# A two-layer feed-forward kernel behind local attention: the second layer's operand tiles get gaps of 32 to 192 bytes between them

## The chip, the cores and the metric

The kernel runs on one core of a Trainium2 chip. The metric is the device time of one execution in microseconds (us); lower is better. Engines go by the short names of the profile: PE is TensorE's matmul, PEld its load of the stationary operand, DVE VectorE, ACT ScalarE, POOL GpSimd, SP SyncE (it issues the DMAs).

## The reference

Local attention with a few global keys (2 sequences of 768 positions, 8 heads of 64), then two feed-forward layers on 1536 tokens of 512 features. Cut to what matters here:

```
x   = attention(q, k, v)                    # 1536 x 512, causal, 96 local and 8 global keys
h   = x @ w_in                              # 512 -> 1024
s   = h * softmax(h)
x   = layernorm(s) * g_ln @ w_out           # 1024 -> 512, the first layer
xn  = x / rms(x) * rms_g
out = (silu(xn @ w_gate) * (xn @ w_val)) @ w2_out    # 512 -> 1536 -> 512, the second layer
```

All is float32. The weights arrive as 64-bit floats and are made into float32 on the core, by bit operations.

## The kernel before, in words

The tokens go through in 12 units of 128 rows. Attention and the first layer run unit by unit, software-pipelined: an order written out by hand in a long string starts it off, and `slot` goes on with it. From about 242 us the second layer alone is left, with tokens in three groups of four units (`GRP` = 4, `NG` = 3), so that a group is 512 tokens wide.

To keep float32 accuracy, each operand is split into a high part that TensorE's faster float32r form holds, and a low part that is the rest: three matmuls, high x high, high x low and low x high, stand in place of one. So each tile comes as a pair: `xgh`/`xgl` (normalized tokens of a group, transposed), `w2hi`/`w2lo` (a slice of second-layer weights: gate, value and output), `ahi`/`alo` (the activated product).

The second layer: `gate_val(f, g)` multiplies weight slice f (12 of them) with token group g: 2 x 4 x 3 = 24 matmuls of 512 columns at L628. There the `w2` block of 128 columns is the stationary operand and `xg` the moving one. ACT takes a tanh of the gate, DVE two products (`th`), ACT rounds `th` to `ahi`, and POOL subtracts to get `alo`. `out_mm(f, g)`, one step later, multiplies the result with the output weights: 4 x 3 = 12 matmuls of 512 columns at L652, here with blocks of `ahi`/`alo` stationary and `w2` moving. With 12 slices and 3 groups that is 36 x 36 = 1296 matmuls. Slices go in three sweeps of four; the weights of the next ones are loaded (`ws`), converted (`wc`) and split meanwhile.

The order on PE is the order of the code (`manual_schedule`). A matmul's stationary block is loaded while the matmul before it streams its moving operand.

Where tiles lie in a partition is set by pools, stacked from two sides: the left stack grows upward, the right one downward. Nearly every tile is a multiple of 512 bytes long, so tiles that follow each other start at the same remainder mod 512. Only constants and small statistics tiles (`p_st`) shift it, and three pads (`PAD_G`, `PAD_X`, `PAD_R`) shift it back. By the sizes in the code, in the kernel before every operand tile of both layers, left and right, starts at remainder 32 mod 512; `ident`, the moving operand of the transposes, starts at 128. A block within a tile starts a multiple of 512 bytes from the tile's start. The pool `p_xg` on the left holds groups 0 and 1, whose space serves earlier as staging of first-layer weights (`wsh`, `wsl`, `wch`, `wcl`); `p_xg2`, `p_ws`, `p_wc`, `p_a` and `p_w2a` (weight slices 0 and 1) lie on the right, where attention's tiles were; `p_w2b` (the other slices) lies on the left, where the first layer's weights were.

Of the kernel before, what the change touches and what calls it, by code (L numbers as in the profile page):

```python
# [12 lines left out]
F32 = mybir.dt.float32  # L13
F32R = mybir.dt.float32r
BF16 = mybir.dt.bfloat16
I32 = mybir.dt.int32
U32 = mybir.dt.uint32
# [5 lines left out]
P = 128  # L23
# [4 lines left out]
KD = DM // P  # L28
# [5 lines left out]
GRP = 4  # L34
NG = NU // GRP
# [1 line left out]
NLOC = 97  # L37
SWEEPS = [4, 4, 4]
MASK = 1.0e12
PAD_G, PAD_X, PAD_R = 128, 384, 448  # L40
LEAD = 1
LAG = 2
DLAG = 3
# [60 lines left out]
CW = 512  # L104
# [14 lines left out]
class Kernel:  # L119
# [485 lines left out]
        self.w2[f] = (hi, lo)  # L605

    def alloc_group(self, g, pool):
        self.xg[g] = [
            pool.tile([P, KD, GRP * P], F32R, tag=f"xg{t}{g}", name=f"xg{t}{g}") for t in ("h", "l")
        ]  # L610

    def silu_mul(self, a, g, v):
        nc = self.nc
# [4 lines left out]
    def gate_val(self, f, g, parts=(0, 1)):  # L618
        nc = self.nc
        xh, xl = self.xg[g]  # L620
        wh, wl = self.w2[f]
        for t in parts:
            pp = self.ps.tile([P, GRP * P], F32, tag=("h", "s")[t], name="gv")
            n = 0
            for k in range(KD):
                c = slice((t * KD + k) * P, (t * KD + k + 1) * P)
                for w, a in ((wh, xh), (wh, xl), (wl, xh)):
                    nc.tensor.matmul(pp, w[:, c], a[:, k, :], start=(n == 0), stop=(n == 3 * KD - 1))  # L628
                    n += 1
            self.gv[f, g, t] = pp  # L630
        if 1 not in parts:
            return
        th = self.p_a.tile([P, GRP * P], F32, tag="th", name="th")
        self.silu_mul(th, self.gv.pop((f, g, 0)), self.gv.pop((f, g, 1)))
        hi = self.p_a.tile([P, GRP * P], F32R, tag="ahi", name="ahi")
        lo = self.p_a.tile([P, GRP * P], F32R, tag="alo", name="alo")
        self.split(hi, lo, th, nc.gpsimd)
        self.act[f, g] = (hi, lo)
# [37 lines left out]
    def fast(self):  # L676
        tc, nc = self.tc, self.nc
        self.qk, self.v, self.p, self.xps, self.x = {}, {}, {}, {}, {}
        self.h, self.hst, self.ln, self.lT, self.xn = {}, {}, {}, {}, {}
        self.eps, self.gv = {}, {}  # L680
        self.sp, self.sst, self.w1, self.lps = {}, {}, {}, {}
        self.w2, self.act, self.acc, self.xg, self.pT = {}, {}, {}, {}, {}
        with ExitStack() as top:
            en = top.enter_context
            pools = {t: en(tc.tile_pool(name="ps_" + t, bufs=n, space=PSUM)) for t, n in BANKS.items()}
            self.ps = Banks(pools)
            self.pad(top, "left", PAD_G)
            self.p_xg = en(tc.tile_pool(name="p_xg", bufs=1, side="left"))
            self.early = (
                [self.p_xg.tile([P, 2, CW, 2], U32, tag=f"xg{t}0", name=f"ws{t}") for t in ("h", "l")],  # L690
                [self.p_xg.tile([P, 4, CW], U32, tag=f"xg{t}1", name=f"wc{t}") for t in ("h", "l")],
            )
            self.n_early = 0
            self.p_st = en(tc.tile_pool(name="p_st", bufs=DLAG + 1, side="left"))
            self.pad(top, "left", PAD_X)
            self.p_xn = en(tc.tile_pool(name="p_xn", bufs=2, side="left"))
            w1x = en(ExitStack())
            atx = en(ExitStack())
            we = w1x.enter_context
            ae = atx.enter_context  # L700
            self.p_w1 = we(tc.tile_pool(name="p_w1", bufs=1, side="left"))
            self.p_x = we(tc.tile_pool(name="p_x", bufs=LEAD + 1, side="left"))
            self.p_e = we(tc.tile_pool(name="p_e", bufs=LAG + 1, side="left"))
            self.p_sq = we(tc.tile_pool(name="p_sq", bufs=1, side="left"))
            self.p_l = we(tc.tile_pool(name="p_l", bufs=2, side="left"))
            self.pad(top, "right", PAD_R)
            self.p_bias = ae(tc.tile_pool(name="p_bias", bufs=1, side="right"))
            self.p_v = ae(tc.tile_pool(name="p_v", bufs=2, side="right"))
            self.p_qk = ae(tc.tile_pool(name="p_qk", bufs=4, side="right"))
            self.p_p = ae(tc.tile_pool(name="p_p", bufs=4, side="right"))  # L710
            self.p_pt = ae(tc.tile_pool(name="p_pt", bufs=4, side="right"))
            self.phase1()
            with tc.manual_schedule(engines={mybir.EngineType.PE}):
                atx.close()
                w2x = en(ExitStack())
                right = lambda n, b: w2x.enter_context(tc.tile_pool(name=n, bufs=b, side="right"))
                self.alloc_group(NG - 1, right("p_xg2", 1))
                self.p_ws = right("p_ws", 2)
                self.p_wc = right("p_wc", 2)
                self.p_a = right("p_a", 2)  # L720
                self.p_w2a = right("p_w2a", 2)
                self.phase2(w1x, w2x)
            w2x.close()
# [346 lines left out]
```

## Time and profile before

| | |
|---|---|
| median of 3 runs | 561.47 us (558.71 to 561.99) |
| profiled execution, its time | 558.16 us |
| its span, first to last instruction | 556.3 us |
| PE busy | 527.8 us, 95% of the span |
| granted TensorE clock, mean | 0.990 |
| matmuls of the second layer | 1296 of 512 columns |

The profile is that of one execution. The time is some 1.9 us longer than the span. A matmul's own duration (some 0.39 us for 512 columns) is a latency, of which the next matmul hides a part; the pace of PE is read from the starts of matmuls that follow each other.

### The profile page before, as it was taken

The numbers are of one execution on the slowest core, as the hardware profiler recorded it, in microseconds if no ns is written. First come the engines' busy times: TensorE is split into PE (matmuls) and PEld (weight loads), VectorE is DVE, ScalarE is ACT, GpSimd is POOL, SyncE is SP. The second block draws the span as 40 slices with busy tenths as digits, with TensorE's granted clock in tenths as the row PEclk, the third lists the DMA queues.
The fourth block names the chain that finished last, engine by engine and source line by source line (L and its number), as shares of the span: only waits on it lengthen the run. The fifth ranks groups of instructions, "written<-read, shape, count | busy, mean of one in ns | idle before, by whom it ended". The sixth has DMA issues, their size and how long they took to land.

```text
span 556.3 us, 7639 instructions
## 1 busy us (share of the span) xinstructions
PE 527.8 (95%) x2736; PEld 424.1 (76%) x2736; DVE 333.4 (60%) x797; ACT 236.6 (43%) x557; POOL 179.0 (32%) x207
## 2 busy tenths in 40 slices
PE   4788989999999999999998999999999999999994
PEld 3466767777877878888886888888888887888883
DVE  6989999776577558975787121673213788231312
ACT  5678767664466456643434121431112434111110
POOL 4874243311331232313544110541111545211010
PEclk9979999999999999999999999999999999999998
DMA  8864712231131022330444000240000242020202
GB/s 290 254 240 142 247 31 67 95 95 47 51 94 39 1 76 77 115 113 16 140 148 151 1 0 1 75 151 1 1 0 1 75 151 77 0 77 0 77 0 82
DMA packets 16670, 45.93 MB, mean 83 GB/s; under 512 B 1904, under 2 KB 2928, under 8 KB 16624
## 3 DMA queue, kind: packets, MB, share of 16 engines
q1 hardware_dynamic: 16624, 45.36, 24.3%
q8 instruction: 23, 0.38, 0.3%
q14 instruction: 23, 0.19, 0.1%
HBM read 42.21 MB, written 3.15 MB: 82 GB/s over the span
## 4 chain that ended last, share of the span: by engine, by line
PE 70%; DVE 20%; POOL 4%; ACT 3%; issue 2%; DMA 1%; POOLq 0%; DVEq 0%; ACTq 0%; SPq 0%
PE gv L628 30%; PE op L652 15%; PE yp L558 11%; PE hp L473 8%; DVE p L278 3%; DVE e L505 2%; POOL p L300 2%; PE tp L316 2%; DVE hst L481 2%; DVE wc L392 1%; PE xps L338 1%; DVE wc L390 1%; DVE xlo L356 1%; PE tp L587 1%; DVE llo L224 1%
## 5 line engine op out<-in xcount | busy, mean ns | idle before, releaser
L628 PE MATMUL gv<-xgh,w2hi 128*128 128x512 f32 x288 | 112.2, 390 | 0.0
L628 PE MATMUL gv<-xgl,w2hi 128*128 128x512 f32 x288 | 112.0, 389 | 0.0
L628 PE MATMUL gv<-xgh,w2lo 128*128 128x512 f32 x288 | 112.0, 389 | 0.0
L224 POOL TENSOR_TENSOR alo<-th,ahi 128x512 fp32r<-128x512 f32 x36 | 47.6, 1322 | 169.9 <-ACT ahi L223 169.8
L300 POOL TENSOR_SCALAR p<-p,ast 128x256 f32<-128x256 f32 (+1 forms) x96 | 56.7, 608 | 103.5 <-DVE ast L282 67.5
L615 DVE SCALAR_TENSOR_TENSOR th<-th,gv 128x512 f32<-128x512 f32 x36 | 24.7, 685 | 100.0 <-ACT th L614 99.9
L224 POOL TENSOR_TENSOR w2lo<-wc,w2hi 128x512 fp32r<-128x512 f32 x36 | 49.0, 1366 | 63.3 <-ACT w2hi L223 63.3
L473 PE MATMUL hp<-win,xhi 128*128 128x512 f32 x192 | 66.0, 407 | 0.7 <-ACT xhi L218 0.7
L628 PEld LDWEIGHTS gv<-xgh,w2lo 128*128 128x128 f32 x288 | 54.1, 188 | 11.3
L628 PEld LDWEIGHTS gv<-xgl,w2hi 128*128 128x128 f32 x288 | 54.1, 188 | 11.2
L628 PEld LDWEIGHTS gv<-xgh,w2hi 128*128 128x128 f32 x288 | 54.1, 188 | 11.0
L558 PE MATMUL yp<-wout,lhi 128*128 128x512 f32 x192 | 60.9, 398 | 0.3 <-DVE wout L456 0.3
L652 PE MATMUL op<-w2hi,alo 128*128 128x512 f32 x144 | 56.4, 392 | 2.3 <-POOL alo L224 2.3
L223 ACT ACTIVATE ahi<-th 128x512 fp32r<-128x512 f32 x36 | 22.7, 631 | 82.7 <-DVE th L616 82.7
L652 PE MATMUL op<-w2hi,ahi 128*128 128x512 f32 x144 | 56.2, 391 | 1.4 <-ACT ahi L223 1.4
L614 ACT ACTIVATE th<-gv 128x512 f32<-128x512 f32 x36 | 21.3, 591 | 82.1 <-PE gv L628 82.1
L652 PE MATMUL op<-w2lo,ahi 128*128 128x512 f32 x144 | 56.1, 389 | 0.0
L289 ACT ACTIVATE p<-p,ast 128x256 f32<-128x256 f32 (+1 forms) x96 | 45.9, 480 | 7.2 <-DVE ast L282 4.0
L473 PEld LDWEIGHTS hp<-win,xhi 128*128 128x128 f32 x192 | 37.1, 193 | 9.1 <-ACT xhi L218 1.4
L616 DVE SCALAR_TENSOR_TENSOR th<-th,gv 128x512 f32<-128x512 f32 x36 | 24.6, 684 | 30.1 <-PE gv L628 29.9
L558 PEld LDWEIGHTS yp<-wout,lhi 128*128 128x128 f32 x192 | 34.9, 188 | 7.3 <-DVE wout L456 0.8
L473 PE MATMUL hp<-win,xlo 128*128 128x512 f32 x96 | 38.7, 403 | 0.4 <-DVE xlo L356 0.4
(118 smaller groups left out, 909.6 us busy)
## 6 DMA issues: line engine op xcount, KB each, us to landing
ws<-in_w SPq DMA_DIRECT2D x36, 512.0 KB, 3.3
qk<-in_qk SPq DMA_DIRECT2D x20, 384.0 KB, 3.8
v<-in_v SPq DMA_DIRECT2D x10, 512.0 KB, 4.1
out_dram<-acc SPq DMA_DIRECT2D x12, 256.0 KB, 3.0
wsh<-in_w_in SPq DMA_DIRECT2D x4, 512.0 KB, 5.3
wsl<-in_w_in SPq DMA_DIRECT2D x4, 512.0 KB, 5.9
wsh<-in_w_out SPq DMA_DIRECT2D x4, 512.0 KB, 3.9
wsl<-in_w_out SPq DMA_DIRECT2D x4, 512.0 KB, 4.5
```

The lines of the kernel that those rows point to most:

```text
L223: self.nc.scalar.activation(out=hi, in_=src, func=AF.Copy)
L224: lo_eng.tensor_tensor(lo, src, f32(hi), ALU.subtract)
L278: nc.vector.tensor_tensor_reduce(pt[:, i, 0:W], sp[h2][:, pl, :], bias[:, 4 * hh + i, :], 1.0, -3.0e38, ALU.add, ALU.max, st[:, 0, i:i + 1],)
L289: self.nc.scalar.activation(out=pt[:, i, 0:W], in_=pt[:, i, 0:W], func=AF.Exp, scale=0.125, bias=st[:, 1, i:i + 1], accum_out=st[:, 2, i:i ...
L300: nc.gpsimd.tensor_scalar(pt[:, i, 0:W], pt[:, i, 0:W], st[:, 3, i:i + 1], 0.0, ALU.mult, ALU.add)
L473: nc.tensor.matmul(hp, a[:, k, :], self.win[w][:, k, c], start=(n == 0), stop=(n == len(mms) - 1))
L558: nc.tensor.matmul(yp, a[:, k, :], self.wout[w][:, k, :], start=(k == 0 and n == 0), stop=(k == KF - 1 and n == 2),)
L614: nc.scalar.activation(out=a, in_=g, func=AF.Tanh, scale=0.5)
L615: nc.vector.scalar_tensor_tensor(out=a, in0=a, scalar=1.0, in1=g, op0=ALU.add, op1=ALU.mult)
L616: nc.vector.scalar_tensor_tensor(out=a, in0=a, scalar=0.5, in1=v, op0=ALU.mult, op1=ALU.mult)
L628: nc.tensor.matmul(pp, w[:, c], a[:, k, :], start=(n == 0), stop=(n == 3 * KD - 1))
L652: nc.tensor.matmul(self.ops[t], a[:, c], w[:, c0], start=(first and n == 0), stop=(last and n == 2))
```

## The change

No instruction, no DMA and no order is changed; only places are. `PAD_G` grows by 32 bytes, and in `p_xg` each of the four tiles is followed by an unused tile of 64 bytes; `PAD_X` shrinks by 288, so that everything to the left stack's end from `p_xn` on (the first layer's tiles and `p_w2b`) lies where it lay. In `p_xg2` a gap of 32 bytes follows `xgh2` and one of 192 follows `xgl2`. In `p_a` two gap tiles, of 32 bytes in each of two buffers, stand between `th`, `ahi` and `alo`. The pools on the right that are placed after `p_xg2` move down with these.

```diff
-PAD_G, PAD_X, PAD_R = 128, 384, 448
+PAD_G, PAD_X, PAD_R = 160, 96, 448
...
     def alloc_group(self, g, pool):
-        self.xg[g] = [
-            pool.tile([P, KD, GRP * P], F32R, tag=f"xg{t}{g}", name=f"xg{t}{g}") for t in ("h", "l")
-        ]
+        self.xg[g] = []
+        for t in ("h", "l"):
+            self.xg[g].append(pool.tile([P, KD, GRP * P], F32R, tag=f"xg{t}{g}", name=f"xg{t}{g}"))
+            if g == NG - 1:
+                pool.tile([P, 8 if t == "h" else 48], F32, name=f"gap{t}{g}")
...
+        if not self.act:
+            self.p_a.tile([P, 8], F32, tag="gap0", name="gap0")
         hi = self.p_a.tile([P, GRP * P], F32R, tag="ahi", name="ahi")
+        if not self.act:
+            self.p_a.tile([P, 8], F32, tag="gap1", name="gap1")
         lo = self.p_a.tile([P, GRP * P], F32R, tag="alo", name="alo")
...
-            self.early = (
-                [self.p_xg.tile([P, 2, CW, 2], U32, tag=f"xg{t}0", name=f"ws{t}") for t in ("h", "l")],
-                [self.p_xg.tile([P, 4, CW], U32, tag=f"xg{t}1", name=f"wc{t}") for t in ("h", "l")],
-            )
+            early = []
+            for i, (n, shape) in enumerate((("ws", [P, 2, CW, 2]), ("wc", [P, 4, CW]))):
+                for t in "hl":
+                    early.append(self.p_xg.tile(shape, U32, tag=f"xg{t}{i}", name=n + t))
+                    self.p_xg.tile([P, 16], F32, name=f"gap{t}{i}")
+            self.early = early[0:2], early[2:4]
```

By the sizes, the remainders mod 512 are then: `xgh0` 64, `xgl0` 128, `xgh1` 192, `xgl1` 256, `xgh2` 320, `xgl2` 352; `ws` and `wc` 320; `th` 192, `ahi` 256, `alo` 320; `w2hi` and `w2lo` of slices 0 and 1 192, of the ten other slices 32 as before.

## Rows read from the trace of the kernel before

**Rows 1.** The page: busy time by engine, then the chain by engine and line.
```profile
PE 527.8 (95%) x2736; PEld 424.1 (76%) x2736; DVE 333.4 (60%) x797; ACT 236.6 (43%) x557; POOL 179.0 (32%) x207
...
PE 70%; DVE 20%; POOL 4%; ACT 3%; issue 2%; DMA 1%; POOLq 0%; DVEq 0%; ACTq 0%; SPq 0%
PE gv L628 30%; PE op L652 15%; PE yp L558 11%; PE hp L473 8%; DVE p L278 3%; DVE e L505 2%; POOL p L300 2%; PE tp L316 2%; DVE hst L481 2%; DVE wc L392 1%; PE xps L338 1%; DVE wc L390 1%; DVE xlo L356 1%; PE tp L587 1%; DVE llo L224 1%
```

**Rows 2.** Windows: busy us of each engine (instructions), granted clock, DMA.
```profile
core 0: us, PE busy (x) PEld busy (x) DVE busy (x) ACT busy (x) POOL busy (x), PEclk, DMA share, GB/s
...
300.00:460.00 160.00, 160.00 (x707) 132.54 (x706) 71.08 (x97) 42.83 (x73) 44.85 (x34) 1.00 0.14 47
462.00:548.00 86.00, 85.58 (x377) 70.84 (x378) 28.16 (x41) 16.39 (x27) 18.53 (x15) 1.00 0.09 32
242.00:300.00 58.00, 55.71 (x250) 45.18 (x249) 40.93 (x59) 24.60 (x45) 24.18 (x19) 1.00 0.33 108
```

**Rows 3.** The chain in order of time, second layer: start us, us, what.
```profile
308.10 5.44 PE gv L628 x24
313.54 2.72 PE op L652 x12
```

**Rows 4.** Timeline at 400 us: start us, us, engine, line, what.
```profile
400.19 0.39 PE L628 MATMUL gv<-xgh,w2lo 128*128 128x512 f32 x1
400.19 0.19 PEld L628 LDWEIGHTS gv<-xgh,w2hi 128*128 128x128 f32 x1
400.42 0.39 PE L628 MATMUL gv<-xgh,w2hi 128*128 128x512 f32 x1
```

**Rows 5.** Timeline of PE from 21 us, the first layer's first wide matmuls.
```profile
21.07 0.63 PE L473 MATMUL hp<-win,xhi 128*128 128x512 f32 x1
...
23.20 0.63 PE L473 MATMUL hp<-win,xlo 128*128 128x512 f32 x1
```

**Rows 6.** The chain from 210 to 300 us, transposes and conversions.
```profile
221.01 0.87 PE tp L540 x8
...
257.29 2.53 POOL w2lo L224 x2
...
274.39 1.67 DVE wc L392
```

**Rows 7.** Timeline of PE, wide matmuls after transposes.
```profile
40.45 0.39 PE L473 MATMUL hp<-win,xlo 128*128 128x512 f32 x1
...
42.06 1.07 PE L473 MATMUL hp<-win,xhi 128*128 128x512 f32 x4
...
101.92 0.40 PE L558 MATMUL yp<-wout,llo 128*128 128x512 f32 x1
...
104.00 0.39 PE L558 MATMUL yp<-wout,llo 128*128 128x512 f32 x1
```

**Rows 8.** Waits of PE from 242 us: us in total, times, longest.
```profile
PE op L652 <- POOL alo L224: 2.3, 2, 1.3
PE op L652 <- ACT ahi L223: 1.4, 1, 1.4
```

**Rows 9.** Tile views (duration min/median/max ns, first and last start us), SP's timeline.
```profile
L263 PE MATMUL sB<-qk x24: 376/376/480, 153.2 to 195.0; 64*128 64x256 f32 x24
...
195.37 38.56 SPq L378 DMA_DIRECT2D ws<-in_w  x7
...
L316 PE MATMUL tp<-ident,p x24: 272/273/328, 190.0 to 209.7; 128*128 128x128 f32 x24
...
L218 ACT ACTIVATE wc<-ws x36: 642/668/699, 211.3 to 468.1; 128x512 f32<-128x512 f32 x36
...
L338 PE MATMUL xps<-pT,v x50: 272/273/323, 189.8 to 211.5; 128*64 128x128 f32 x50
...
L224 POOL TENSOR_TENSOR w2lo<-wc,w2hi x18: 1287/1296/1507, 218.8 to 297.3; 128x512 fp32r<-128x512 f32 x18
```

**Rows 10.** Groups by line from 300 to 460 us: busy us, mean ns, idle before.
```profile
L224 POOL TENSOR_TENSOR alo<-th,ahi 128x512 fp32r<-128x512 f32 x19 | 25.0, 1317 | 98.4 <-ACT ahi L223 98.4
```

## The prediction, made before the changed kernel ran

> **What bounds the kernel now.** I read the page first, its busy shares and the chain [rows 1]: PE is busy 95% of the span, and the chain that ends last is PE for 70%, with the two matmul lines of the second layer (L628 and L652) as its largest pieces, 45% together. Then the windows [rows 2]: from 300 to 460 us PE is never idle, from 462 to 548 us for 0.4 us, with the granted clock at 1.00, while DVE, ACT and POOL are busy less than half of the time. So in these 246 us the time is a number of matmuls times the pace of one. From 242 to 300 us PE is busy 55.7 of 58 us, but the conversion of weights keeps up only just: DVE is busy 41 us there, and the chain runs through conversions on DVE and POOL [rows 6]. The waits of PE in the second layer come to 3.7 us in all [rows 8].
>
> The pace is the number to look at. In the chain 24 matmuls of L628 take 5.44 us and 12 of L652 take 2.72 us [rows 3]: 226.7 ns each in both. 512 columns at one a cycle of 2.4 GHz are 213.3 ns, so each matmul pays 13.3 ns on top. A change that adds no instruction can do something only to these 13.3 ns, or to a wait.
>
> What happens during one: the stationary block of the next matmul is loaded from the moment this one starts, 0.19 us long [rows 4]. So two streams read the memory at once, the moving tile (2048 bytes of each partition) and the stationary block (512 bytes). In the kernel before, both begin at the same remainder mod 512 in every wide matmul of both layers: their distance is 0. That is the property that the change takes away in the second layer.
>
> **The change part by part.** *Instructions, DMAs, order:* none is added, removed or moved, so that costs nothing by itself. The gap tiles are written and read by nobody, so nobody waits for them.
>
> *Places reused.* The right-hand pools move down by up to 352 bytes and so lie over somewhat other tiles of attention, whose last readers they wait for. The second buffer of `ws` now also touches one more `qk` buffer: the last score matmul started at 195.0 us, the first load of `ws` was issued at 195.37, behind it in any case [rows 9]. The second `wc` touches one more `p` buffer: last read at 209.7 us, first `wc` written at 211.3, so a cover of 1.6 us. The second `w2lo` touches one more `pT`: last read at 211.5, first `w2lo` written at 218.8. All three are covered; the thinnest cover is the first, and were it gone it would delay a load that the core has 16 us to wait for, until ACT reads it at 211.3. I take 0. The statistics tiles move by 288 bytes; they feed no wide matmul: 0.
>
> *Engines other than PE.* POOL's subtraction reads `th` and `ahi`, 0 apart before and 64 after. It takes 1317 ns, and POOL sat idle 98 us of the 160 before it, waiting for `ahi` [rows 10]. Its least and largest durations in the like operation on weights are 1287 and 1507 ns [rows 9], so the bounds are -0.03 and +0.2 us per step, and the step has 8.16 us (5.44 + 2.72). Off the path from 300 us on; from 242 to 300 us it could move the waits of 3.7 us either way, by 0.2 us for each of three: 0.6 us, inside the error. I take 0.
>
> *The pace of the wide matmuls.* This is the term. The new distance of the moving tile from the stationary block mod 512: for the ten slices of `w2` at 32, `gate_val` has 32 and 96 in group 0, 160 and 224 in group 1, 288 and 320 in group 2; `out_mm` has 288 (`ahi`) and 224 (`alo`). For the two slices at 192 they are 384, 448, 0, 64, 128, 160, and 448 and 384. So 32 of the 1296 pairs (slices 0 and 1 with `xgh1`, 16 each) still stand at 0 and nearly all others get another distance.
>
> No row shows a wide matmul at a distance other than 0, so I bound it from both sides. The lower end: transposes are the one long-running matmul whose operands lie apart (`ident` at 128, the data at 32: distance 96). Eight in a row take 0.87 us [rows 6], 108.8 ns for 128 columns that evidently take two cycles each (106.7 ns): only 2.1 ns on top. With 2.1 instead of 13.3 ns a wide matmul would take 215.4 ns, 11.3 less. That they stream at half the rate weakens this: in the first layer's first wide matmuls, which come 0.426 us apart (five steps from 21.07 to 23.20 us, [rows 5]) and so at half the rate too, distance 0 costs nothing either (512 columns at 1.2 GHz are 426.7 ns). What the two rows together say is that the 13.3 ns are no fixed cost of an instruction: they appear only when the moving stream runs at full rate, as a collision of two streams would.
>
> The upper end: the same instruction at the same distance isn't always at 226.7. Behind transposes or a wait PE takes a handful of slower steps before it settles: seven steps from 40.45 to 42.06 us are 230 ns each, nine from 101.92 to 104.00 are 231 [rows 7], with single steps reading up to 0.24 us. So the cost depends on how the two streams stand to each other in time, which is another sign of a collision, and distance 0 has a state that they fall into and keep.
>
> The count: matmuls that set the time are the 707 and 377 of the two windows [rows 2], 1084. Those from 242 to 300 us gain nothing, as the conversions would be late next; but a slower pace there would be paid, so a loss counts all 1296.
>
> I take the middle between 215.4 and 226.7, 221.0 ns: a collision that most of the new distances avoid in part, since nothing in the trace tells the nine distances apart. That is 5.65 ns x 1084 = 6.1 us less. Against the profiled execution's 558.16 us: 552.0. That execution is 3.3 us below the median of 561.47, so for a median I add 3.3: 555.4 us, a gain of 1.1%. A measurement of this kernel tells about 1% from no change. What is late next: the sweeps' conversions of weights, whose POOL steps gave PE its waits; with 2.5% less time between a weight buffer's release and its use (two steps, 16 us) the waits grow by some 0.4 us, inside the range. The ends: all of the 11.3 ns gone gives 12.2 us less, 549.2 on the median.
>
> **The rivals.** *No change (561.5 us).* The 13.3 ns belong to the float32r form at full rate, or the two streams meet equally often at any distance: the stationary stream covers exactly 512 bytes, so whatever the offset, it passes each remainder once. For it: the pace is the same 226.7 in L628 and L652, with tiles far apart or near, on both sides of the memory [rows 3]. Against it: at half rate the cost is gone [rows 5], and behind a restart it is larger [rows 7]. The Trainium skill speaks for this rival: "SBUF — State Buffer", section "Who interferes with whom", gives PE two independent read ports, one for the moving operand and one for the load of weights, and says that PE never waits on anyone. By that rule the change would be worth nothing. The rows don't agree fully: the pace differs between like instructions by 4 ns. Its "TensorE: Matmul & The Clock Gate", section "Wait — 56ns, not 53.3ns?", states a cost of about 2.5 ns on a warm matmul, 215.7 ns for 512 columns in bf16; the rows have 226.7, so 11 ns more in this form. With 215.7 as the end reached, the sum would be 11.9 us less, close to my own lower end.
>
> *Slower (567 us).* The settled state of 226.7 ns needs the same distance from one matmul to the next. After the change `gate_val` goes 32, 96, 32, 32, 96, 32 and so on, so each third matmul stands differently to its neighbour, and PE stays in the unsettled state of [rows 7], at 231.1 ns: 4.4 x 1296 = 5.7 us more, 567.2 on the median. Its place is L628 first, where distances alternate; it decides if the steps at 300 to 460 us are not even. With 0.24 us, the largest single reading, it would be 17 us more. For it: the settling is in the rows, and the layout of before is one in which nothing differs from step to step. Against it: it is not shown that a differing distance, rather than the restart alone, keeps PE from settling.
>
> *The change doesn't do what it says* (a gap tile could make a later step wait, or not move what it should) would leave the time at 561.5 and is part of the first rival.
>
> **How the numbers follow.** Forecast 0.43, no change 0.30, slower 0.27. Of the forecast 0.38 lies beyond 1% (below 555.9) and 0.05 within, as the gain may be a part of the middle value. Of the slower case 0.25 lies beyond 1% (above 567.1), since its price reaches up to 17 us, and 0.02 within. So faster 0.38, within 1% 0.37, slower 0.25. The forecast alone would span 549 to 559. For 8 in 10 the range has to take in no change and the near part of the slower case: from 547 (the full gain, and 2 us for the spread of the runs) to 570 (the slower case at 233 ns). That leaves out about 0.04 below and 0.13 above.
>
> **What would show it.** Right: in the chain from 300 us on the 24 matmuls of L628 take 5.30 us instead of 5.44 and the 12 of L652 take 2.65 instead of 2.72, with different values for the three groups if the distances differ in effect; the first layer's pace stays at 226.7 (its tiles keep distance 0); busy times of DVE, ACT and POOL stay. No change: 5.44 and 2.72 again. Slower: 5.5 and more for L628 and uneven steps within a run of 24. What would make the prediction wrong beyond these: a collision that depends on distance so sharply that some of the nine distances are far worse than 0, so that one group gains and another loses; or a cost on DVE or POOL that moves conversions onto the path before 300 us.

## The result and the profile after

The changed kernel takes 564.18 us in the median of 8 runs (563.01 to 565.23), the kernel before, run beside it, 560.77 us (8 runs, 558.17 to 561.99). The ratio is 1.0069 with a 95% interval of 1.0043 to 1.0094: slower by 0.7%, by an amount that the interval keeps apart from nothing and below 1%. The forecast was 1.1% faster: the sign is wrong.

Times of either kernel fall into two clusters some 2 us apart (before 558.2 to 558.9 and 560.1 to 562.0, after 563.0 to 563.5 and 564.9 to 565.2), which is why the two profiled executions, both of the lower cluster, differ by 5.1 us (558.16 and 563.22) but the medians by 3.4: before, the median lies in the upper cluster, after, between the two.

The page of the changed kernel: busy time by engine, then the chain by engine and by line.

```profile
PE 534.0 (95%) x2736; PEld 424.4 (76%) x2736; DVE 334.0 (59%) x797; ACT 236.5 (42%) x557; POOL 180.4 (32%) x207
...
PE 66%; DVE 22%; POOL 4%; ACT 4%; issue 2%; DMA 1%; POOLq 0%; ACTq 0%; DVEq 0%; SPq 0%
PE gv L630 27%; PE op L658 14%; PE yp L558 11%; PE hp L473 8%; DVE p L278 3%; DVE wc L392 2%; POOL p L300 2%; DVE e L505 2%; DVE wc L396 2%; PE tp L316 2%; DVE wc L390 2%; PE xps L338 1%; ACT wc L218 1%; DVE hst L481 1%; DVE xlo L356 1%
```

Against [rows 1], the same 2736 matmuls keep PE busy 6.2 us longer; DVE, ACT and POOL are within 1.4 us of before. The chain's shares mislead here: PE's part falls from 70 to 66%, as the chain steps off PE onto weight conversions between 434 and 462 us. The windows show that PE was not waiting there (160.00 of 160 us busy up to 460 us, and 28.00 of 28 us from 434 to 462). Their columns are us, then busy us (instructions) of PE, PEld, DVE, ACT and POOL, granted clock, DMA share, GB/s.

```profile
300.00:460.00 160.00, 160.00 (x691) 129.56 (x690) 68.33 (x92) 41.52 (x70) 44.35 (x33) 1.00 0.13 44
462.00:548.00 86.00, 85.31 (x368) 68.74 (x367) 30.21 (x44) 17.36 (x29) 19.50 (x15) 1.00 0.10 37
242.00:300.00 58.00, 56.33 (x249) 45.19 (x249) 40.67 (x58) 24.68 (x45) 24.24 (x19) 1.00 0.33 109
```

The first row has the main reading: at the same granted clock of 1.00, with PE busy all the time, 691 matmuls fit into the 160 us where 707 did [rows 2]. The chain in order of time says the same of single runs of matmuls (start us, us, what).

```profile
221.24 0.87 PE tp L540 x8
...
333.69 5.54 PE gv L630 x24
339.24 2.77 PE op L658 x12
...
350.33 5.58 PE gv L630 x24
355.91 2.77 PE op L658 x12
...
383.75 5.63 PE gv L630 x24
389.38 2.77 PE op L658 x12
```

L630 and L658 are the old L628 and L652. Where [rows 3] has 5.44 and 2.72 us throughout, 24 matmuls of `gate_val` now take 5.58 us in group 0 (350 us), 5.63 in group 1 (383 us) and 5.54 in group 2 (333 us): 232.5, 234.6 and 230.8 ns each. `out_mm` takes 2.77, 230.8 ns each, behind all three. The eight transposes still take 0.87 us, as in [rows 6].

A single step hardly shows this. In the timeline of PE, five steps of group 1 take 1.17 us, 234 ns each, while the duration of one stays 0.39 to 0.40 us as in [rows 4]: the pace is in the starts.

```profile
383.82 0.40 PE L630 MATMUL gv<-xgl,w2hi 128*128 128x512 f32 x1
...
384.99 0.39 PE L630 MATMUL gv<-xgh,w2hi 128*128 128x512 f32 x1
```

Last, PE's waits from 242 us on (us in total, times, longest), and, for 300 to 460 us as in [rows 10], the group of POOL's subtraction (busy us, mean ns, idle time before).

```profile
PE op L658 <- POOL alo L224: 1.6, 2, 0.9
PE op L658 <- ACT ahi L223: 0.7, 1, 0.7
```

```profile
L224 POOL TENSOR_TENSOR alo<-th,ahi 128x512 fp32r<-128x512 f32 x19 | 25.1, 1321 | 101.3 <-ACT ahi L223 101.3
```

The waits fell from 3.7 us [rows 8] to 2.3: with PE slower, POOL and ACT are late by less. The subtraction takes 1321 ns where it took 1317 [rows 10].

The account of the profiled pair, from the starts in the two traces: 1285 steps from one matmul of the second layer to the next (those without a wait, under 280 ns) take 6.9 us more than at 226.7 ns each; in the kernel before it is 0.2 us more, over 1282 steps. The waits give back 1.4. From the start of the first matmul of `gate_val` to that of the last of `out_mm` the trace has 311.4 us (242.90 to 554.33) where it had 306.3 (242.65 to 548.93), 5.1 us more. That is the whole difference of the two profiled executions: what lies ahead of this stretch is longer by 0.25 us, what lies behind it shorter by 0.3.

### The profile page after: what moved, and what is told of

The parts are those of the page before. It is cut to its first block, busy times and chain, and to the rows that moved or that the text cites. A ratio compares the mean times of both kernels' runs of the same rounds, so it can differ in the third digit from the quotient of the medians.

```text
span 561.4 us, 7639 instructions
## 1 busy us (share of the span) xinstructions
PE 534.0 (95%) x2736; PEld 424.4 (76%) x2736; DVE 334.0 (59%) x797; ACT 236.5 (42%) x557; POOL 180.4 (32%) x207
## 4 chain that ended last, share of the span: by engine, by line
PE 66%; DVE 22%; POOL 4%; ACT 4%; issue 2%; DMA 1%; POOLq 0%; ACTq 0%; DVEq 0%; SPq 0%
PE gv L630 27%; PE op L658 14%; PE yp L558 11%; PE hp L473 8%; DVE p L278 3%; DVE wc L392 2%; POOL p L300 2%; DVE e L505 2%; DVE wc L396 2%; PE tp L316 2%; DVE wc L390 2%; PE xps L338 1%; ACT wc L218 1%; DVE hst L481 1%; DVE xlo L356 1%
## 5 line engine op out<-in xcount | busy, mean ns | idle before, releaser
L630 PE MATMUL gv<-xgh,w2lo 128*128 128x512 f32 x288 | 113.8, 395 | 0.0
L630 PE MATMUL gv<-xgl,w2hi 128*128 128x512 f32 x288 | 113.7, 395 | 0.0
L630 PE MATMUL gv<-xgh,w2hi 128*128 128x512 f32 x288 | 113.7, 395 | 0.0
L630 PEld LDWEIGHTS gv<-xgh,w2hi 128*128 128x128 f32 x288 | 54.2, 188 | 12.6
L630 PEld LDWEIGHTS gv<-xgh,w2lo 128*128 128x128 f32 x288 | 54.1, 188 | 12.8
L630 PEld LDWEIGHTS gv<-xgl,w2hi 128*128 128x128 f32 x288 | 54.0, 188 | 12.8
L658 PE MATMUL op<-w2hi,alo 128*128 128x512 f32 x144 | 56.8, 395 | 1.6 <-POOL alo L224 1.6
L658 PE MATMUL op<-w2hi,ahi 128*128 128x512 f32 x144 | 56.9, 395 | 0.7 <-ACT ahi L223 0.7
L658 PE MATMUL op<-w2lo,ahi 128*128 128x512 f32 x144 | 56.4, 392 | 0.0
```

Source lines behind the costliest of these rows:

```text
L658: nc.tensor.matmul(self.ops[t], a[:, c], w[:, c0], start=(first and n == 0), stop=(last and n == 2))
```

## The experiments

The distance below is that of a matmul's moving tile from its stationary one. The theories, from the forecast's pieces and the slower rival's:

- *Same distance:* PE settles at 226.7 ns at any distance, if it stays the same from matmul to matmul.
- *Pair:* what counts is the distance of the moving tile to the one block that is read at the same time, which is the next matmul's stationary block.
- *All congruent:* every operand tile has to lie at the same remainder, mod 512 or a part of it.

All kernels but two are the kernel before with a helper that puts an unused tile behind a named one, and a list of gaps; `PAD_G` and `PAD_X` keep the first layer's tiles at their remainder.

```diff
+    def gap(self, pool, after):
+        if GAPS.get(after) and after not in self.gaps:
+            self.gaps.add(after)
+            pool.tile([P, GAPS[after] // 4], F32, tag=f"gap_{after}", name=f"gap_{after}", bufs=1)
...
             self.xg[g].append(pool.tile([P, KD, GRP * P], F32R, tag=f"xg{t}{g}", name=f"xg{t}{g}"))
+            self.gap(pool, f"xg{t}{g}")
```

It is called in the same way behind `w2hi`, `w2lo` (`_a`: slices 0 and 1, `_b`: the others), `th`, `ahi` and `alo`. The first four kernels shared a chip (before: 559.25 us, 7 runs), the next four another (before: 558.79, 25 runs), the last four ran in pairs. Where a kernel ran once, its total is one reading out of a spread of some 4 us (the 25 runs of before: 557.03 to 561.41), so the verdicts go by the chain, whose values for the same group agree to 0.03 us within a run: group 0 stands at 350 us, group 1 at 383, group 2 at 417, for the ten later slices.

### One distance in each group

```diff
-PAD_G, PAD_X, PAD_R = 128, 384, 448
+PAD_G, PAD_X, PAD_R = 160, 256, 448
+GAPS = {'xgl0': 96, 'xgl2': 256, 'alo': 160, 'w2lo_a': 32}
```

High and low tiles at one remainder: distance 32 in group 0, 128 in group 1, 256 in group 2, 416 in `out_mm`.

> High and low tiles of a pair at one remainder, so that the distance of the moving tile from the next stationary block is the same at every step of a run, but not 0: for slices 2 to 11 it is 32, 128 and 256 in groups 0, 1 and 2, and 416 in out_mm. Evenness theory (PE settles whenever the distance is the same from step to step, whatever it is): 226.7 ns in every group and in out_mm, span 556 to 557 us. Distance theory (every distance other than 0 has a cost of its own): 229 to 236 ns, different from group to group, span 560 to 562 us.

562.70 us. The chain:

```profile
350.35 5.59 PE gv L638 x24
355.94 2.80 PE op L665 x12
...
383.93 5.57 PE gv L638 x24
...
417.48 5.46 PE gv L638 x24
```

The second one of the kind, with other distances: 96, 288 and 448 in the groups, 352 in `out_mm`.

```diff
+PAD_G, PAD_X, PAD_R = 224, 96, 448
+GAPS = {'xgl0': 192, 'xgl2': 64, 'alo': 288, 'w2lo_a': 192}
```

> As the run beside it, with distances 96, 288 and 448 in groups 0, 1 and 2 and 352 in out_mm. Evenness theory: 226.7 ns everywhere, span 556 to 557 us. Distance theory: 229 to 236 ns, each distance its own value, span 560 to 562 us. 96 and 288 also stand in the changed kernel, beside another distance: distance theory expects the like pace here.

563.50 us.

```profile
349.93 5.60 PE gv L638 x24
355.53 2.80 PE op L665 x12
...
383.49 5.59 PE gv L638 x24
...
417.09 5.60 PE gv L638 x24
```

*Same distance* fell: at 32, 96, 128, 288, 352, 416 and 448 an unchanging distance is as slow as the mixture, 232.1 to 233.3 ns. Only 256 keeps nearly the old pace (5.46 here; the two runs of group 2 in the first sweep took 5.44): by the starts, the first four steps of the run at 417 us take 229 to 236 ns, the others 226 to 228. So the period may be 256 bytes.

### The pair that is read at the same time

Each moving tile at distance 0 from the block that is loaded while it streams, in group 0 and in `out_mm`; at 64 in group 1, at 448 in group 2.

```diff
+PAD_G, PAD_X, PAD_R = 128, 256, 448
+GAPS = {'xgh0': 64, 'xgh1': 64, 'xgh2': 64, 'ahi': 64, 'alo': 384, 'w2hi_a': 64, 'w2hi_b': 64}
```

> Each low tile (xgl, w2lo, alo) 64 bytes further than its high one. The moving tile then stands at one and the same distance from the stationary block that is loaded meanwhile (that of the next matmul): 0 in group 0 and out_mm of slices 2 to 11, 64 in group 1, 448 in group 2; but successive moving tiles, successive stationary blocks, and a matmul's own two operands stand differently from step to step. Evenness theory for the pair that is read at the same time: 226.7 ns everywhere, ratio 1.000 to the kernel before. If the distance itself counts: 226.7 in group 0 and out_mm, 229 to 236 in groups 1 and 2. If another pair counts (own operands, or a tile and its successor): 229 to 235 everywhere, ratio 1.005 to 1.01.

564.01 us median, ratio 1.0094 (1.0064 to 1.0124).

```profile
352.16 5.55 PE gv L638 x24
357.71 2.77 PE op L665 x12
...
385.44 5.59 PE gv L638 x24
...
418.91 5.60 PE gv L638 x24
```

*Pair*, alone, fell: group 0 and `out_mm` take 231.2 and 230.8 ns with every such pair at distance 0.

### The change without its gaps in `p_a`

`th`, `ahi` and `alo` back to the remainder of `w2`; the `xg` tiles as in the change. A gap behind `alo` brings the `w2` tiles of slices 0 and 1 back too.

```diff
+PAD_G, PAD_X, PAD_R = 160, 96, 448
+GAPS = {'xgh0': 64, 'xgl0': 64, 'xgh1': 64, 'xgl1': 64, 'xgh2': 32, 'xgl2': 192, 'alo': 288}
```

> The changed kernel's gaps between the xg tiles alone; th, ahi, alo and all w2 at remainder 32 as before, so that out_mm is at distance 0. Both theories of the pair: out_mm at 226.7 ns again, gate_val of slices 2 to 11 at 232.5, 234.7 and 231.0 ns in groups 0, 1 and 2 as in the changed kernel, so 4.9 us more PE time than before instead of 6.9, and a span of 559 to 560.5 us, ratio 1.004 to 1.007. If the cost is one of the whole layout instead (other engines, staging): out_mm is slow too, or gate_val fast.

562.03 us median, ratio 1.0059 (1.0036 to 1.0083).

```profile
352.00 5.57 PE gv L638 x24
357.58 2.72 PE op L665 x12
385.18 5.61 PE gv L638 x24
390.79 2.72 PE op L665 x12
...
418.51 5.60 PE gv L638 x24
```

`out_mm` is back at 226.7 ns at once, between two runs of `gate_val` that are not. So each of the two lines pays by its own tiles. The steps of the second layer lose 5.6 us against 226.7 ns here, where 4.9 was expected, and 6.9 us in the whole change.

### Distances 0 and 256 in turn

In groups 0 and 2 and in `p_a` one half of a pair at distance 0 and the other at 256; in group 1 both at 256.

```diff
+PAD_G, PAD_X, PAD_R = 128, 128, 448
+GAPS = {'xgh0': 256, 'xgh2': 256, 'ahi': 256}
```

> Tiles moved by 256 bytes or by none: xgl0, both of group 1, xgh2 and alo lie at 288, all the rest at 32. If the cost repeats every 256 bytes (so read from the equal values at 32 and 288, 64 and 320, 96 and 352, 480 and 224): 226.7 ns everywhere although distances mod 512 differ from step to step, ratio 1.000. If different distances mod 512 in themselves keep PE unsettled: 229 to 235 ns in groups 0 and 2 and in out_mm, 226.7 in group 1 at most, ratio 1.004 to 1.008.

559.64 us median, ratio 1.0005 (0.9979 to 1.0031).

```profile
350.97 5.44 PE gv L638 x24
356.41 2.72 PE op L665 x12
383.61 5.44 PE gv L638 x24
```

In the first two rows the distance mod 512 differs from matmul to matmul, in the third it is 256 throughout, and nothing is lost in either. What counts is the distance mod 256. Mod 256 these tiles are no mixture, so this run does not say what a mixture costs by itself; a later one does (`xgl` moved alone).

### Three more distances

160, 64 and 384 in groups 0, 1 and 2; 256 in `out_mm`.

```diff
+PAD_G, PAD_X, PAD_R = 288, 320, 448
+GAPS = {'xgl0': 416, 'xgl2': 128, 'alo': 128}
```

> High and low at one remainder again; for slices 2 to 11 the distances are 160, 64 and 384 in groups 0, 1 and 2 and 256 in out_mm; for slices 0 and 1 they are 416, 320, 128 and 0. A cost that repeats every 256 bytes: 64 gives 229 as two steps of slices 0 and 1 had it, 384 gives 232.6 as 128 did, 256 and 0 give 226.7, 160 gives some 233 to 234 as 416 had it in out_mm. If the number of the slice or the kind of matmul counted rather than the distance, out_mm would stay at 231 to 234.

562.07 us.

```profile
333.75 5.59 PE gv L638 x24
...
350.41 5.62 PE gv L638 x24
356.02 2.73 PE op L665 x12
383.79 5.51 PE gv L638 x24
389.30 2.77 PE op L665 x12
```

Group 2 stands at 333 us here. With the first two kernels, the pace at one distance, mod 256:

| distance mod 256 | 24 of `gate_val`, us | ns each |
|---|---|---|
| 0 | 5.44 | 226.7 |
| 32 | 5.59, 5.59 | 232.9 |
| 64 | 5.51 | 229.6 |
| 96 | 5.60 | 233.3 |
| 128 | 5.57, 5.59 | 232.1, 232.9 |
| 160 | 5.62 | 234.2 |
| 192 | 5.60 | 233.3 |

Two distances that differ by 256 have one row (32 and 288: 5.59 and 5.59; 128 and 384: 5.57 and 5.59). `out_mm` at 256 takes 2.73 us behind group 0 and 2.77 behind group 1: after a run at another distance the 12 matmuls don't always settle at once. By the starts, behind group 0 the first two steps take 232 and 231 ns and the others 226 to 227; behind group 1 the first ten take 224 to 236, and only the last two 226 and 227. At distance 0 there was no such delay behind slow runs (2.72 in the kernel without gaps in `p_a`). So 256 has the pace of 0 once PE has settled; why it settles later is open.

### All tiles moved together

The three pads alone, so that all operand tiles of both layers start at remainder 0 in place of 32.

```diff
-PAD_G, PAD_X, PAD_R = 128, 384, 448
+PAD_G, PAD_X, PAD_R = 96, 384, 480
```

> The kernel before with every tile of both layers moved by 32 bytes, so that all lie at remainder 0 instead of 32. If only distances between tiles count: 226.7 ns everywhere and ratio 1.000. If the place in a 64-byte line counts as well, the pace moves, up or down, in both layers.

559.24 us median, ratio 1.0008 (0.9984 to 1.0032).

```profile
398.21 5.44 PE gv L628 x24
403.65 2.72 PE op L652 x12
```

Of the two places tried, 0 and 32, neither is better; the distances count.

### The transposes at distance 0

`ident`, the moving tile of the transposes, moved from remainder 128 to 32. This tests the forecast's lower end.

```diff
-PAD_G, PAD_X, PAD_R = 128, 384, 448
+PAD_G, PAD_X, PAD_R = 224, 384, 448
...
+        const.tile([P, 104], F32, name="pad_ident")
         self.ident = const.tile([P, P], F32, name="ident")
```

> The kernel before with the moving operand of the transposes at remainder 32 too, instead of 128, so that their distance to the data is 0 and no longer 96. If a jump of the moving tile's remainder is what unsettles PE, the slower steps behind transposes (230 to 236 ns, five to nine of them) go, some 0.7 us over the first 242 us, and they stay where PE had waited; transposes stay at 109 ns. If any restart unsettles PE, nothing changes. Time within 0.2% of before in both cases.

557.96 us median, ratio 0.9998 (0.9974 to 1.0022).

```profile
223.12 0.88 PE tp L541 x8
...
235.38 0.87 PE tp L541 x8
```

Eight transposes take 0.87 to 0.88 us at distance 0 as they took 0.87 at distance 96. So that row said nothing about what distance does to a wide matmul. The slower steps behind transposes [rows 7] stay as well: above 226.7 ns, the first layer's wide matmuls lose 0.84 us in all here and 0.74 in the kernel before. So it is not where `ident` lies that unsettles PE. That any restart does is the reading that is left; it was not tested by itself.

### One kind of tile alone, by 128 bytes

The last four kernels move one of the four kinds of tile and leave the others congruent mod 256. In `gate_val` `xg` moves and `w2` stands still; in `out_mm` `w2` moves and `a` stands still. So each kernel gives one reading for either role.

```diff
+PAD_G, PAD_X, PAD_R = 128, 384, 448
+GAPS = {'w2hi_a': 128, 'w2lo_a': 128, 'w2hi_b': 128, 'w2lo_b': 128}
```

> Only the low halves of the second layer's weights (w2lo) are moved, by 128 bytes mod 256 from everything else; all moving tiles and w2hi stay congruent mod 256. In a run of 24 of gate_val the order is xgl with w2hi, xgh with w2lo, xgh with w2hi, so one matmul in three reads a stationary tile at distance 128. Theory A (each matmul pays for the distance of its moving tile to its own stationary block, or to the one that is loaded meanwhile): only one in three pays; 24 take 5.44 + 8 x 6 ns = 5.49 us (228.7 ns each), and 562 us is not reached: about 561. Which one of the three is slow tells own from next: the one that uses w2lo, or the one ahead of it. Theory B (one tile off breaks the settled state for all): the whole run is at 231 ns or more, 24 take 5.54 us or more, about 563 to 564 us.

563.10 us, beside one execution of the kernel before at 561.38.

```profile
351.64 5.55 PE gv L638 x24
357.19 2.75 PE op L665 x12
```

The counterpart, `xgl` and `alo`:

```diff
+PAD_G, PAD_X, PAD_R = 128, 384, 448
+GAPS = {'xgh0': 128, 'xgl0': 128, 'xgh1': 128, 'xgl1': 128, 'xgh2': 128, 'xgl2': 128, 'ahi': 128, 'alo': 128}
```

> The counterpart: only the low halves of the moving tiles (xgl in all three groups, and alo) are moved, by 128 bytes mod 256; w2hi, w2lo, xgh and ahi stay congruent mod 256. One matmul in three (xgl with w2hi) has a moving tile at distance 128, to its own stationary block and to the next one alike. Theory A: as in the run with w2lo alone, one in three pays: 24 take about 5.49 us, the total is about 561. Theory B: the whole run is at 231 ns or more, 24 take 5.54 us or more, 563 to 564 us. If this run pays and the one with w2lo alone does not, it is the moving stream's change of place from one matmul to the next that counts; the other way round, the stationary one's.

561.32 us.

```profile
350.31 5.49 PE gv L638 x24
355.80 2.77 PE op L665 x12
```

Theory B fell, although the run with `w2lo` has its numbers (5.55 and 563.10): a tile that is off is paid for by some steps, and the others keep their pace. From the starts in the trace, means from 305 to 460 us: with `w2lo` moved, the step of `xgh` with `w2hi` takes 226.7 ns, that of `xgl` with `w2hi` (while `w2lo` is loaded) 232.4, that of `xgh` with `w2lo` 234.2. With `xgl` moved, only its own step is slow, 234.2; the other two take 226.7 and 225.8, although the distance of the moving tile changes from step to step. So a mixture does not slow the steps that are at distance 0. Theory A has the 5.49 of `xgl`, but not the 5.55 of `w2lo`, where two steps in three pay and not one. That suggested theory C of the next two runs.

The high tiles `xgh` and `ahi` (for this and the next, gaps also stand ahead of the first tile of a pair, `pre_`):

```diff
+PAD_G, PAD_X, PAD_R = 256, 384, 448
+GAPS = {'xgh0': 128, 'xgl0': 128, 'xgh1': 128, 'pre_xg2': 128, 'xgh2': 128, 'th': 128, 'ahi': 128}
```

> Only the high halves of the moving tiles (xgh in all three groups) and ahi are moved, by 128 bytes mod 256. Theory C, from the two runs before: a matmul pays about 6.5 ns when its moving tile stands apart from its own stationary block or from the one that is loaded meanwhile. In gate_val (xgh with w2hi, xgl with w2hi, xgh with w2lo) that is two in three, the ones that read xgh: 24 take 5.55 us. In out_mm, where ahi is the stationary tile of two in three, it is all three: 12 take 2.79 to 2.80 us. Theory E: only the alternation of places within one stream counts; then this run has the same as the one with xgl and alo alone, 5.49 and 2.77 us.

561.88 us, beside one execution of the kernel before at 559.49.

```profile
350.38 5.50 PE gv L640 x24
355.88 2.79 PE op L667 x12
```

And `w2hi`:

```diff
+PAD_G, PAD_X, PAD_R = 128, 384, 448
+GAPS = {'pre_w2_a': 128, 'w2hi_a': 128, 'pre_w2_b': 128, 'w2hi_b': 128}
```

> Only the high halves of the second layer's weights (w2hi) are moved, by 128 bytes mod 256. Theory C: in gate_val all three matmuls pay (xgh with w2hi: own; xgl with w2hi: own; xgh with w2lo: the next one, w2hi, is loaded meanwhile): 24 take 5.58 to 5.60 us. In out_mm, where w2hi is the moving tile of two in three and the stationary tiles stay congruent, two in three pay: 12 take 2.77 us. Theory E: as in the run with w2lo alone, 5.55 and 2.75 us.

562.07 us.

```profile
350.00 5.58 PE gv L640 x24
355.58 2.75 PE op L667 x12
```

Neither theory holds as a whole: C has two of the four values (2.79 and 5.58) and misses two (5.50 for 5.55, 2.75 for 2.77); E has those that C misses (5.49 and 2.75) and misses the other two. Sorted by role, the eight values are plain; the nanoseconds are the chain's time over 24 or 12, less 226.7:

| tile that is off | as moving tile | as stationary tile |
|---|---|---|
| low half (read by one matmul in three) | `xgl` 5.49 us: +2.1 ns; `w2lo` 2.75 us: +2.5 ns | `w2lo` 5.55 us: +4.6 ns; `alo` 2.77 us: +4.2 ns |
| high half (read by two in three) | `xgh` 5.50 us: +2.5 ns; `w2hi` 2.75 us: +2.5 ns | `w2hi` 5.58 us: +5.8 ns; `ahi` 2.79 us: +5.8 ns |

With one kind of tile off, a stationary one costs about twice what a moving one does. For a moving tile it hardly matters which half is off; of the stationary ones the high half costs 1.2 to 1.6 ns more. `gate_val` and `out_mm` agree within 0.4 ns in each cell (the chain's last digit, 0.01 us, is 0.4 ns of one and 0.8 ns of the other). By the steps it is a matter of how many pay: a low stationary half slows two steps in three, the one that loads it and the one that uses it (`w2lo` 232.4 and 234.2 ns, `alo` 232.6 and 234.1), a low moving half its own alone (`xgl` 234.2, `w2lo` 234.1). A high stationary half slows all three (232.1 to 233.9), a high moving half its own two, mostly by less (228.5 to 232.8). The costs don't add up: with both halves of `xg` at 128 (the first kernel, group 1) it is +5.4 ns, and at that distance it is the same to call the moving tiles off or the stationary ones.

## Why the prediction was wrong

*What bounds the kernel* was right. The second layer's time is the number of matmuls times their pace: PE is busy 160.00 of 160 us before and after, and 691 in place of 707 matmuls is the result.

*The terms at zero* were right. Instructions and DMAs are the same; POOL's subtraction changed by 4 ns, inside the bounds of -30 and +200; the first layer's pace stayed (its wide matmuls lose 0.70 us above 226.7 ns after the change, 0.74 before); DVE, ACT and POOL are busy as long as before.

*The 13.3 ns as a collision of the moving and the stationary stream* is not shown. That the pace depends on how the two lie to each other is, by the table of distances and by the four kernels with one kind of tile moved; but these are a further 2 to 8 ns. No layout has a run of matmuls with a pace clearly below 226.7 ns, so the 13.3 stayed in all of them, and they may be a cost of the form at full rate, as the first rival had it. The argument against a fixed cost rested on rows at half rate, which would read the same if such a cost were hidden there. What meets inside the memory is not shown either.

*The step that failed* is "I take the middle between 215.4 and 226.7, 221.0 ns: a collision that most of the new distances avoid in part". The mean step measured 232.0 ns (226.7 + 6.9 us over 1285 steps), 11 ns above that: the term of 5.65 ns less was 5.35 ns more. Distance 0, which the text took for the costly case, is the best of those tried, and none of the six others in the table goes below it. The lower end, 215.4 ns, came from eight transposes at distance 96. The run with `ident` moved shows that these cost the same at distance 0, so the row carried no information on distance. (The distances that the text counts as nine are ten; no sum goes by that.) The sum's interval lay wholly on the gain's side, as the upper end was the pace of before; the slower steps of [rows 7], which stood right beside it in the text, were given to a rival and not to the bound. Since, as the text says, no row shows a wide matmul at a distance other than 0, the interval had to hold 226.7 inside it, with at least 231 as its upper end. The measured 564.18 us lies inside the range of 547 to 570 only because the rivals had stretched it; the forecast by itself spanned 549 to 559.

*The slower rival* was right in sign and place: L630 first, uneven steps (225 to 238 ns within group 0's runs), different values for the three groups. Its price of 4.4 ns x 1296 = 5.7 us was a little low: 5.3 x 1296 is 6.9. It came out at 5.1 net, as the waits on `alo` and `ahi` fell by 1.4 us. The rival let the loss count for all 1296 matmuls with nothing given back; here the slower PE also gave its suppliers time. Its reason was half right. It said that PE needs the same distance from step to step. The runs say that this is not enough (distances of 32 or 96 throughout: 232.9 and 233.3 ns), and that steps at distance 0 keep their pace beside others that are off (with `xgl` moved alone: 226.7 and 225.8 beside 234.2). Of the distances tried, only 0 mod 256 has the pace of before.

*No change* fell, 5.44 us against 5.54 to 5.63 with the same instructions. The Trainium skill's "SBUF — State Buffer", section "Who interferes with whom", by which PE with its two read ports waits on no one, doesn't describe this form: the same matmul takes 226.7 or 234.6 ns by where its operands lie. The figure in its "TensorE: Matmul & The Clock Gate", section "Wait — 56ns, not 53.3ns?", 215.7 ns for 512 columns in bf16, was reached by no layout; the lowest pace over a whole run here is 226.7.

*What stays open.* Why 64 is cheaper (229.6 ns) than its neighbours 32 and 96; why a high moving half, read by two steps in three, costs no more than a low one; which accesses meet; how 224 does by itself, which stood only beside 160; and whether distances that are no multiple of 32 bytes behave alike, which wasn't tried. No layout tried beats the kernel before: those at its pace (all at 0 mod 256) have ratios of 0.9998 to 1.0008, all with 1 inside the interval.

## What to carry to other kernels

Where long runs of float32r matmuls set the time, try to give all their operand tiles, moving and stationary, the same start mod 256 bytes; here this was worth 2 to 8 ns of some 230 ns per matmul, and of the two common remainders tried, 0 and 32, neither was better. Where not all can be, stationary tiles come first: one kind of them alone off by 128 bytes cost 4.2 to 5.8 ns per matmul, one kind of moving tile 2.1 to 2.5. And when a row of the trace is to bound a cost, ask whether it would have read otherwise with the property changed; if that is not known, let the bounds reach to both sides of the present value.

## What the runs showed of the hardware that was not expected

- The pace of a 512-column float32r matmul with a 128x128 stationary block depends on the distance of its operands mod 256 bytes: 226.7 ns at 0, 229.6 at 64, 232.1 to 234.2 at 32, 96, 128, 160 and 192. 256 has the pace of 0 once PE has settled, which behind a run at another distance took two to ten steps.
- The common remainder made no difference: all tiles at 0 or all at 32 gave 5.44 us for 24.
- A tile that is off slows the steps that touch it and can leave the rest alone: with `xgl` moved by 128 bytes, its own step took 234.2 ns and the other two 225.8 and 226.7.
- Behind transposes or a wait PE takes some slower steps before it settles, whether the transposes ahead of it are at distance 0 or 96 (0.84 and 0.74 us lost in the first layer).
- The granted clock fell from 1.00 to 0.50 (2.4 to 1.2 GHz) for a stretch that began between 298.6 and 300.7 us in the traces of three kernels (0 and 256 in turn, `ident` moved, `w2lo` moved), just behind PE's waits for `ahi` and `alo`; seven steps there take 426 to 427 ns, and 1.5 to 1.6 us are lost. The length of the waits doesn't decide it: with `w2lo` moved they were 0.90 and 0.93 us, while the kernel before had 1.36 and 0.94 us in the same place and kept 1.00.
